# Seven-product matrix multiplies in a fused attention and FFN block: one operand of the second weight made later, and partial sums of the first product kept in PSUM

## The chip, the cores and the metric

The kernel runs on 1 core of one Trainium2 chip. The metric is the device time in microseconds (us) of one launch; it includes everything from the first load to the last store. A time is given as the median of several runs.

## What is computed

The reference is a block on a sequence of 2048 tokens of width 576, all in float32. Its inputs are normalized per token; one branch is linear attention with 32 heads of width 18, the other an FFN with a hidden width of 4608, and the branches are multiplied:

```python
xn = _layernorm(x)
q, k, v = split(xn @ wqkv)                  # 32 heads of width 18
phi = lambda t: where(t > 0, t + 1, exp(t)) + 1e-6
kv = einsum("bhsd,bhse->bhde", phi(k), v);  z = phi(k).sum over tokens
s = ((phi(q) @ kv) / (phi(q) . z + 1e-6)) @ wo
h = gelu(xn @ w1 + b1)                      # 576 -> 4608
g = silu(h @ w2 + b2)                       # 4608 -> 576
out = x + s * g
```

Most of the work, and the whole change, lies in the two FFN products `xn @ w1` and `h @ w2`.

## The kernel before, in words

**Float32 from pairs.** A matrix operand `t` is kept as a high part `hi`, a rounded copy of `t` in TensorE's fast float32 format, and a low part `lo = t - hi`. A product takes three matmuls: hi·hi, hi·lo, lo·hi. The high part is made by ScalarE (`set_hi`, L812, a cast; in the first stage `w2_hi`, L413), the low part by VectorE (`set_lo`, L815; for the first weight L874; in the first stage `w2_lo`, L418). Below, such a step is called a *cast* or *split*.

**Seven products in place of eight.** Both FFN products are cut into blocks of two by two and multiplied by a scheme of Strassen's kind: seven products M1 to M7 of sums of blocks, and additions on the results. Operands that are sums (of the inputs, the weights or the hidden values) are made by POOL, in place.

**Stages.** In the first stage (to about 150 us) the keys and values are projected, one tile of 128 tokens after the other (loop over `t`, 16 tiles), and in the gaps some operands of the weights are made and stored to DRAM: `w2_load`, `w2_sum`, `w2_hi`, `w2_lo`, `w2_store` (L392 to L423) make operands 5 and 6 of the second weight (`T_OPS`) for all 9 chunks. POOL makes the sum (L405), ScalarE the high part (L413), VectorE the low part (L418), and SP's queue stores both (L423). The second stage (to 283 us) does the queries and the attention output.

**The FFN stage** has 18 steps of the loop at L1511, called chunks here: 9 chunks of 512 hidden columns for the first half of the tokens, and the same 9 for the second half. In the first half the weights' operands are made and stored to DRAM; in the second they are loaded. A chunk has two *pairs* (class `Up`, L1129, each for 256 hidden columns and 1024 tokens) and then the down products (`product`, L1273). The very last chunk ends with plain products instead (`down_plain`, L1386).

**A pair** calls `step(i)` for the products in the order `UP` (L1453): 1, 6, 7, 5, 2, 3, 4. Each product is 7 matmuls of 512 columns (`mm`, L1140). Its results go through PSUM:

- `bank1` tiles (pool `psum1`, two buffers of one bank): `a` and `e`. `bank2` tiles (pool `psum`, three buffers of two banks): `b` and `zy`; only one bank of `b` is used.
- M1 goes to `a`; ScalarE copies it to SBUF (`m1_sb`, L1164). Later M2 adds onto it in `a`.
- VectorE makes `u1 = M6 + M1` (L1167) and `u2 = M7 + u1` (L1170) in SBUF, then M5 + u2 (L1173), M3 + M5 + u1 (L1180; M3 adds onto M5 in `e`) and M4 + u2 (L1184) in PSUM.
- Four GELUs by ScalarE (`gelu`, L1155) read the four sums and write the hidden blocks to SBUF. The block of the last GELU (`gelu(0, 1, ...)`) is needed for sums 7 and 5 of the second product's operands.

**The down products** run in the order 1, 2, 7, 4, 5, 3, 6 (`ORDER`), each as two *groups* of 12 matmuls of 288 columns on a `bank2` tile. M2 adds onto M1's tile, M4 onto M7's and M3 onto M5's, and VectorE adds each tile to the accumulator `macc` (L1292). So a chunk takes 4 + 8 = 12 `bank2` tiles from the three buffers, always in the same places: `b` and `zy` of the first pair take buffers 0 and 1, those of the second 2 and 0, the two groups of the first down product take 1 and 2, the next 0.

**Order of the work.** `in_order` (L59, entered at L1509) fixes VectorE, ScalarE, POOL and TensorE to the order in which the program issues instructions; SP's queue of DMAs is not named there. After each step of a pair and each group `at_step` (L1495) issues what the tables have planned for that step. A chunk has 28 steps (`NS`): 0 to 6 the first pair, 7 to 13 the second, 14 to 27 the groups. In the first half, `P1` and `P0` plan the first weight's operands; `PW2` (L1475) plans the high parts of the second weight's operands (2 at step 0, 1 at 1, 7 at 3, 4 at 5, 3 at 8), with the low part and the store to DRAM (`keep_op`, L806) one step later, and POOL's `sum7` (L1199) at step 0 and two `sum4` (L1202) at step 2. Operands 5 and 6 are loaded at steps 23 and 27 of the chunk before. `PH` (L1479) plans sums (POOL), high and low parts of the second product's left operands, made from the GELUs' blocks; the first of them are planned from step 7 on, beside the second pair. POOL's sums, the casts and the splits of one chunk thus share queues with the additions and the GELUs of its pairs. At the change from the first half to the second, three SiLU activations of accumulators (L1362) are planned for the first two steps.

Of the kernel before, what the change touches and what calls it, by code (L numbers as in the profile page):

```python
# [8 lines left out]
F32 = mybir.dt.float32  # L9
F32R = mybir.dt.float32r  # L10
# [5 lines left out]
P = 128  # L16
S = 2048
D = 576
HD = 288
# [25 lines left out]
def linear_attention_gated_ffn(ctx, tc, x, xT, wqkv, wo, w1, w1e, b1, w2, b2, out):  # L45
    nc = tc.nc
    SUB, MUL, ADD = ALU.subtract, ALU.mult, ALU.add
# [34 lines left out]
    def bank2(name):  # L82
        return psum.tile([P, 2, 512], F32, tag="pp", name=name)

    def bank1(name):
        return psum1.tile([P, 512], F32, tag="p1", name=name)
# [36 lines left out]
    w1_dram, w2_dram = {}, {}  # L123
# [262 lines left out]

    T_OPS = (5, 6)
    w2raw, w2op = {}, {}  # L390

    def w2_load(c):  # L392
        t = w2p.tile([P, 3, 2, HD], F32, tag="w2r", name=f"w2r{c}")
        nc.sync.dma_start(t.rearrange("p b a d -> p (b a d)"), w2[c][:, D:])
        w2raw[c] = t

    def w2_block(c, i):

        B11, B00, B01 = (w2raw[c][:, k] for k in range(3))
        return {5: (B00, B01, B00), 6: (B11, B11, B00)}[i]  # L400

    def w2_sum(j):
        c, i = j // 2, T_OPS[j % 2]
        dst, a, b = w2_block(c, i)
        nc.gpsimd.tensor_tensor(dst, a, b, op=SUB)  # L405

    def w2_hi(j):
        shape = [P, 2, 2, HD]
        if j % 4 < 2:
            w2op[j] = stw.tile(shape, F32R, tag="stw", name=f"w2o{j}")  # L410
        else:
            w2op[j] = w2p.tile(shape, F32R, tag="w2o", name=f"w2o{j}")
        nc.scalar.copy(w2op[j][:, 0], w2_block(j // 2, T_OPS[j % 2])[0])  # L413

    def w2_lo(j):
        c, i = j // 2, T_OPS[j % 2]
        t = w2op[j]
        nc.vector.tensor_tensor(t[:, 1], w2_block(c, i)[0], t[:, 0].bitcast(F32), op=SUB)  # L418

    def w2_store(j):  # L420
        c, i = j // 2, T_OPS[j % 2]
        w2_dram[c, i] = d = dram.tile([P, 2, 2, HD], F32, name=f"op_{c}_{i}")
        nc.sync.dma_start(d, w2op.pop(j).bitcast(F32))  # L423

# [32 lines left out]
    WE_SUMS = {2 * q + 1: q for q in range(WG)}  # L457
    W2_AT = (2, 4, 6, 8, 10, 11, 12, 13, 14)
    W2_LOADS = {0: 0, 1: 1, 3: 2, 5: 3, 7: 4, 9: 5, 11: 6, 12: 7, 13: 8}
    W2_SUMS = {t: (2 * c, 2 * c + 1) for c, t in enumerate(W2_AT)}  # L460

    class XSums:

# [18 lines left out]
        def tt(self, out, a, b, op):  # L482
            nc.vector.tensor_tensor(out, a.bitcast(F32), b.bitcast(F32), op=op)
# [24 lines left out]
        def sum4(self, k):  # L508
            self.tt(self.t, (self.h0, self.l0)[k][:, self.B], self.t, (SUB, ADD)[k])
# [615 lines left out]

    mid = md.tile([P, 5, 512], F32, name="mid")
    m1_sb, u1_sb, u2_sb = (mid[:, i] for i in range(3))

    class Up:  # L1129


        def __init__(self, n, w, xs):
            self.p, self.w = n % NP, w
            self.xb = xs

            self.a, self.b = bank1(f"a{n}"), bank2(f"b{n}")
            self.zy, self.e = bank2(f"zy{n}"), bank1(f"e{n}")
            self.g = {}

        def mm(self, ps, i, first=True):  # L1140
# [15 lines left out]
            self.g[n, b] = g  # L1156

        def step(self, i):
            A, B, E = self.a, self.b[:, 0, :], self.e
            Z, Y = self.zy[:, 0, :], self.zy[:, 1, :]  # L1160
            tt = nc.vector.tensor_tensor
            if i == 1:
                self.mm(A, 1)
                nc.scalar.copy(m1_sb, A)  # L1164
            elif i == 6:
                self.mm(B, 6)
                tt(u1_sb, B, m1_sb, op=ADD)  # L1167
            elif i == 7:
                self.mm(Z, 7)
                tt(u2_sb, Z, u1_sb, op=ADD)  # L1170
            elif i == 5:
                self.mm(E, 5)
                tt(B, E, u2_sb, op=ADD)  # L1173
                self.gelu(1, 1, B)
            elif i == 2:
                self.mm(A, 2, first=False)
                self.gelu(0, 0, A)
            elif i == 3:
                self.mm(E, 3, first=False)
                tt(E, E, u1_sb, op=ADD)  # L1180
                self.gelu(1, 0, E)
            else:
                self.mm(Y, 4)
                tt(Y, Y, u2_sb, op=ADD)  # L1184
                self.gelu(0, 1, Y)


    class W2:
# [10 lines left out]
        def sum7(self):  # L1199
            nc.gpsimd.tensor_tensor(self.src[7], self.src[3], self.src[7], op=SUB)  # L1200

        def sum4(self, k):  # L1202

            self.src[4] = t = self.src[2]
            nc.gpsimd.tensor_tensor(t, t, self.src[(7, 1)[k]], op=SUB)

        def plain(self, f):
            k = 2 - 2 * (f % 2)
# [16 lines left out]
    class HOps:  # L1225
# [224 lines left out]
        if i:  # L1450
            load_rest(0, REST_AT[i], 1, x_new[k][:, 4])

    UP = (1, 6, 7, 5, 2, 3, 4)  # L1453
    NS = 28


# [15 lines left out]
    )  # L1472


    PW2 = {2: 0, 1: 1, 7: 3, 4: 5, 3: 8}  # L1475
    W2_SUMS_NEXT = {5: 23, 6: 27}
    W2_SUMS_FIRST = {5: 6, 6: 10}
    W2_NEXT = {1: 15, 2: 17, 7: 19, 4: 21, 5: 23, 3: 25, 6: 27}
    PH = dict(  # L1479
        S={(7, 0): 7, (5, 0): 8, (6, 0): 11, (3, 0): 11, (7, 1): 13, (5, 1): 14, (6, 1): 15, (3, 1): 15},  # L1480
# [30 lines left out]
    for step in range(n_chunks):  # L1511
# [4 lines left out]
        if half == 0:  # L1516
            plan_w1(add, w1t[2 * step + 1], base, **P1)
            add(base, w2t[step].sum7)
            for k in range(2):
                add(base + 2, w2t[step].sum4, k)  # L1520
            for i, at in PW2.items():
                add(base + at, w2t[step].hi, i)
                add(base + at + 1, w2t[step].lo, i)
            if step == 0:
                for i, at in W2_SUMS_FIRST.items():
                    add(at, w2t[0].load, i)
        change = step == NC - 1
        if not plain:
            add(base + (11 if change else 7), load_we, 2 * step + 2)
# [1 line left out]
        if half == 0 and c < NC - 1:  # L1531
            add(base + 0, make, W1, w1t, 2 * step + 2)
            add(base + 4, make, W1, w1t, 2 * step + 3)
            add(base + 1, lambda n=2 * step + 2, base=base: plan_w1(add, w1t[n], base, **P0))
            make(W2, w2t, step + 1)
            add(base + 22, w2t[step + 1].load_raw)
            for i, at in W2_SUMS_NEXT.items():
                add(base + at, lambda i=i, n=step + 1: w2t[n].load(i))
        elif not plain:
            add(base + (11 if change else 7), make, W1Loaded, w1t, 2 * step + 2)  # L1540
            add(base + (11 if change else 14), load_six, 2 * step + 2)
            add(base + (16 if change else 14), make, W1Loaded, w1t, 2 * step + 3)
# [115 lines left out]
```

## Time and profile before

| | |
|---|---|
| Runs | 1098.13, 1102.75 and 1105.87 us; median 1102.75 us |
| Span of the profiled execution, first to last instruction | 1096.2 us |
| Time around that span, against the runs' median | 6.55 us |
| TensorE clock granted, mean over the span | 0.999 |
| First and second stage | 0 to 283 us |
| Chunks, first half of the tokens | 9, from 283.0 us |
| Chunks, second half of the tokens | 9, from 685.5 us; the last one ends in plain products |
| HBM read and written | 164.24 MB and 95.17 MB |
| DMA packets | 262.54 MB, mean 239 GB/s |

How to read the profile: PE is TensorE's matmuls, PEld its weight loads (they overlap), DVE is VectorE, ACT is ScalarE, POOL is GpSimd, SP is the engine that issues DMAs. `L1164` is line 1164 of the kernel before. A row of groups gives line, engine, operation, output `<-` inputs, shapes and the number of instructions, then busy us and mean ns of one, then the idle time of the engine before them and who ended it. A row of the timeline gives start in us, duration in us, engine, line, operation and tiles, and in brackets the engine's idle time before it. Matmuls are pipelined, so durations of single matmuls overlap; the time of a product is read from the length of a stretch.

### The profile page before, as it was taken

The page shows a single profiled execution, that of the slowest core. Times are in us where ns is not written, and L with a number is a line of the kernel's source. Part 1 is how long each engine was busy: PE and PEld are TensorE (multiplying, and loading weights), DVE is VectorE, ACT ScalarE, POOL GpSimd, SP SyncE. Part 2 cuts the span into 40 slices and gives each one's busy share as a digit, 9 for nine tenths or more (in the row PEclk, how much of TensorE's full clock was granted, in tenths as well). Part 3 has the DMA queues.
Part 4 walks back from the last instruction along what each step waited for, and adds up shares of the span by engine and source line. Part 5 has one row for each costly group of instructions (what it writes and reads, how often), then busy time and mean ns, then how long its engine had stood idle before and what let it go on. Part 6 is the DMA issues. An engine that isn't in the chain of part 4 may idle for free.

```text
span 1096.2 us, 18083 instructions
## 1 busy us (share of the span) xinstructions
PE 1088.2 (99%) x6702; PEld 1008.8 (92%) x6702; DVE 829.5 (76%) x1132; ACT 491.3 (45%) x844; POOL 471.5 (43%) x403
## 2 busy tenths in 40 slices
PE   9999999999999999999999999999999999999998
PEld 8999989999898998989989989899898998989987
DVE  7787748888798888888888888667475584764856
ACT  6555555555545455454453544524234243242442
POOL 3676434323546446464554553424234143242340
PEclk9999999999999999999999999999999999999999
DMA  7898834675959558486585769978676676767452
GB/s 248 264 274 274 309 137 149 206 248 186 333 221 350 182 220 322 160 320 224 189 332 175 284 237 400 391 248 289 215 241 219 210 231 212 238 219 224 126 184 87
DMA packets 88400, 262.54 MB, mean 239 GB/s; under 512 B 11894, under 2 KB 24182, under 8 KB 85624
## 3 DMA queue, kind: packets, MB, share of 16 engines
q1 hardware_dynamic: 88312, 261.38, 69.3%
q8 instruction: 53, 0.87, 0.3%
q14 instruction: 35, 0.29, 0.1%
HBM read 164.24 MB, written 95.17 MB: 237 GB/s over the span
## 4 chain that ended last, share of the span: by engine, by line
PE 99%; DVE 1%; ACT 0%; issue 0%; POOL 0%; DVEq 0%; POOLq 0%
PE pm L1286 35%; PE a L1147 10%; PE e L1147 10%; PE zy L1147 10%; PE pk L321 6%; PE pq L321 5%; PE ps_s L788 5%; PE b L1147 5%; PE pv L321 4%; PE pd L1402 2%; PE ps_kva L382 1%; PE ptp L770 1%; PE ps_kw L707 1%; PE warm L369 0%; DVE wkv_l L364 0%; PE ps_kvb L382 0%
## 5 line engine op out<-in xcount | busy, mean ns | idle before, releaser
L1292 DVE TENSOR_TENSOR macc<-pm,macc 128x576 f32<-128x576 f32 x218 | 163.9, 752 | 49.9 <-PE pm L1286 48.4
L812 ACT CAST h_h<-g 128x512 fp32r<-128x512 f32 x204 | 121.9, 621 | 132.7 <-PE pm L1286 131.5
L815 DVE TENSOR_TENSOR h_l<-g,h_h 128x512 fp32r<-128x512 f32 x204 | 161.8, 800 | 0.0
L1252 POOL TENSOR_TENSOR mid<-g 128x512 f32<-128x512 f32 x34 | 43.9, 1292 | 108.1 <-ACT g L1155 108.1
L1246 POOL TENSOR_TENSOR g<-g 128x512 f32<-128x512 f32 x34 | 54.9, 1616 | 49.5 <-DVE h_l L815 28.4
L1155 ACT ACTIVATE g<-b,b1c 128x512 f32<-128x512 f32 x36 | 24.8, 690 | 102.5 <-DVE b L1173 102.5
L1164 ACT COPY mid<-a 128x512 f32<-128x512 f32 x36 | 21.1, 585 | 95.3 <-PE a L1147 95.3
L858 POOL TENSOR_TENSOR w1raw<-w1raw 128x256 f32<-128x256 f32 x18 | 13.3, 737 | 116.8 <-ACT h_h L812 68.2
L1167 DVE TENSOR_TENSOR mid<-b,mid 128x512 f32<-128x512 f32 x36 | 24.8, 690 | 45.0 <-PE b L1147 41.8
L1374 POOL TENSOR_TENSOR fin1l<-fin1h,fin1l 128x288 f32<-128x288 f32 x8 | 6.5, 811 | 118.4 <-DMA fin1l<-s_dram 69.6
L1249 POOL TENSOR_TENSOR g<-g 128x512 f32<-128x512 f32 x34 | 55.2, 1623 | 2.7
L1147 PE MATMUL a<-h0r,wa 128*128 128x512 f32 x144 | 50.4, 390 | 0.0
L1147 PE MATMUL a<-xh,wa 128*128 128x512 f32 x144 | 50.4, 390 | 0.0
L815 DVE TENSOR_TENSOR h_l<-mid,h_h 128x512 fp32r<-128x512 f32 x34 | 48.8, 1436 | 1.2
L1155 ACT ACTIVATE g<-e,b1c 128x512 f32<-128x512 f32 x36 | 24.8, 690 | 51.9 <-DVE e L1180 51.9
L753 POOL TENSOR_TENSOR pbuf<-phiq,den 128x576 f32<-128x576 f32 x16 | 19.4, 1213 | 63.6 <-DVE den L752 63.6
L1243 POOL TENSOR_TENSOR g<-g 128x512 f32<-128x512 f32 x34 | 44.1, 1296 | 2.7
L1180 DVE TENSOR_TENSOR e<-e,mid 128x512 f32<-128x512 f32 x36 | 24.8, 690 | 22.3 <-PE e L1147 22.3
L1170 DVE TENSOR_TENSOR mid<-zy,mid 128x512 f32<-128x512 f32 x36 | 24.9, 691 | 19.8 <-PE zy L1147 19.8
L1173 DVE TENSOR_TENSOR b<-e,mid 128x512 f32<-128x512 f32 x36 | 25.2, 700 | 18.5 <-PE e L1147 17.4
L321 PE MATMUL pk<-wkv_h,xh 128*128 128x288 f32 (+1 forms) x160 | 38.2, 321 | 0.4 <-ACT xh L248 0.4
L321 PE MATMUL pk<-wkv_l,xh 128*128 128x288 f32 (+1 forms) x160 | 38.4, 321 | 0.0
(857 smaller groups left out, 3646.5 us busy)
## 6 DMA issues: line engine op xcount, KB each, us to landing
we<-we_dram SPq DMA_DIRECT2D x36, 448.0 KB
w2raw<-w SPq DMA_DIRECT2D x10, 1152.0 KB
op<-w2o SPq DMA_DIRECT2D x18, 576.0 KB
w1raw<-w SPq DMA_DIRECT2D x18, 512.0 KB
op_a<-wa SPq DMA_DIRECT2D x18, 512.0 KB
op_c<-wc SPq DMA_DIRECT2D x18, 512.0 KB
op_d<-wd SPq DMA_DIRECT2D x18, 512.0 KB
wc<-op_c SPq DMA_DIRECT2D x18, 512.0 KB
```

Source lines behind the costliest of these rows:

```text
L321: nc.tensor.matmul(ps[:, h, : ws.stop - ws.start], st, w[:, k, ws], start=(begin and i == 0), stop=(end and i == len(seq) - 1), skip_group ...
L788: nc.tensor.matmul(ps[:, h, :HD], st[:, k, :], w[:, k, h * HD : (h + 1) * HD], start=(i == 0), stop=(i == len(seq) - 1),)
L812: nc.scalar.copy(pair[0], src)
L815: eng.tensor_tensor(pair[1], src, pair[0].bitcast(F32), op=SUB)
L1147: nc.tensor.matmul(ps, st, mv, start=first and n == 0, stop=n == len(seq) - 1, skip_group_check=True,)
L1155: nc.scalar.activation(g, ps, AF.Gelu_apprx_tanh, bias=b1c[:, f : f + 1])
L1243: tt(src[5, pr], A(1, 0), A(1, 1), op=ADD)
L1246: tt(src[6, pr], src[5, pr], A(0, 0), op=SUB)
L1249: tt(src[3, pr], A(0, 1), src[6, pr], op=SUB)
L1252: tt(src[7, pr], A(0, 0), A(1, 0), op=SUB)
L1286: nc.tensor.matmul(ps[:, q, :HD], hs[p][st][:, cs], m[:, p, :], start=(n == 0 and i not in CHAIN), stop=(n == 5), skip_group_check=True,)
L1292: nc.vector.tensor_tensor(dst, src, dst, op=ADD)
```

## The change

Two things change. First, operand 6 of the second weight is not made in the first stage any more: the load there takes two blocks instead of three, only operand 5 is made, and one tile tag holds it. Operand 6 is made in the chunks of the first half: POOL makes it as `sum6` from operand 7, in place of a block, operand 4 then takes one subtraction (of operand 6) instead of two, and `PW2` casts 4 at step 6, 6 at step 7 and 3 at step 9. It is stored to DRAM there, and loaded from there in the second half as before.

Second, a pair's products come in the order 1, 2, 6, 5, 7, 3, 4. M6 and M7 add onto M1 in the bank `a`; ScalarE copies the bank after M1, after M6 (`u1`) and after M7 (`u2`), and copies M5 from `e`, into the place of M1's copy. VectorE's additions are four: M2 + m1, (M1+M6+M7) + m5, M3 + M5 + u1, M4 + u2. The `bank2` tiles are `bc` (bank B for M2, bank C for M4) and `z` (written by VectorE alone), in the places of `b` and `zy`.

```diff
     def w2_load(c):
-        t = w2p.tile([P, 3, 2, HD], F32, tag="w2r", name=f"w2r{c}")
-        nc.sync.dma_start(t.rearrange("p b a d -> p (b a d)"), w2[c][:, D:])
+        t = w2p.tile([P, 2, 2, HD], F32, tag="w2r", name=f"w2r{c}")
+        nc.sync.dma_start(t.rearrange("p b a d -> p (b a d)"), w2[c][:, 2 * D :])
...
+    def w2_sum(c):
+        B00, B01 = (w2raw[c][:, k] for k in range(2))
+        nc.gpsimd.tensor_tensor(B00, B01, B00, op=SUB)
...
-    W2_SUMS = {t: (2 * c, 2 * c + 1) for c, t in enumerate(W2_AT)}
+    W2_SUMS = {t: (c,) for c, t in enumerate(W2_AT)}
...
     m1_sb, u1_sb, u2_sb = (mid[:, i] for i in range(3))
+    m5_sb = m1_sb
...
-            self.a, self.b = bank1(f"a{n}"), bank2(f"b{n}")
-            self.zy, self.e = bank2(f"zy{n}"), bank1(f"e{n}")
+            self.a, self.e = bank1(f"a{n}"), bank1(f"e{n}")
+            self.bc, self.z = bank2(f"bc{n}"), bank2(f"z{n}")
...
             if i == 1:
                 self.mm(A, 1)
                 nc.scalar.copy(m1_sb, A)
+            elif i == 2:
+                self.mm(B, 2)
+                tt(B, B, m1_sb, op=ADD)
             elif i == 6:
-                self.mm(B, 6)
-                tt(u1_sb, B, m1_sb, op=ADD)
-            elif i == 7:
-                self.mm(Z, 7)
-                tt(u2_sb, Z, u1_sb, op=ADD)
+                self.mm(A, 6, first=False)
+                nc.scalar.copy(u1_sb, A)
+                self.gelu(0, 0, B)
             elif i == 5:
                 self.mm(E, 5)
-                tt(B, E, u2_sb, op=ADD)
-                self.gelu(1, 1, B)
-            elif i == 2:
-                self.mm(A, 2, first=False)
-                self.gelu(0, 0, A)
-            elif i == 3:
+                nc.scalar.copy(m5_sb, E)
+            elif i == 7:
+                self.mm(A, 7, first=False)
+                tt(Z, A, m5_sb, op=ADD)
+                nc.scalar.copy(u2_sb, A)
+                self.gelu(1, 1, Z)
+            elif i == 4:
+                self.mm(C, 4)
+                tt(C, C, u2_sb, op=ADD)
+                self.gelu(0, 1, C)
+            else:
                 self.mm(E, 3, first=False)
                 tt(E, E, u1_sb, op=ADD)
                 self.gelu(1, 0, E)
-            else:
-                self.mm(Y, 4)
-                tt(Y, Y, u2_sb, op=ADD)
-                self.gelu(0, 1, Y)
...
-        def sum4(self, k):
-
+        def sum6(self):
+            self.src[6] = t = self.src[1]
+            nc.gpsimd.tensor_tensor(t, self.src[7], t, op=ADD)
+
+        def sum4(self):
             self.src[4] = t = self.src[2]
-            nc.gpsimd.tensor_tensor(t, t, self.src[(7, 1)[k]], op=SUB)
+            nc.gpsimd.tensor_tensor(t, t, self.src[6], op=SUB)
...
-    UP = (1, 6, 7, 5, 2, 3, 4)
+    UP = (1, 2, 6, 5, 7, 3, 4)
...
-    PW2 = {2: 0, 1: 1, 7: 3, 4: 5, 3: 8}
-    W2_SUMS_NEXT = {5: 23, 6: 27}
-    W2_SUMS_FIRST = {5: 6, 6: 10}
+    PW2 = {2: 0, 1: 1, 7: 3, 4: 6, 6: 7, 3: 9}
...
-            for k in range(2):
-                add(base + 2, w2t[step].sum4, k)
+            add(base + 3, w2t[step].sum6)
+            add(base + 3, w2t[step].sum4)
...
-            for i, at in W2_SUMS_NEXT.items():
-                add(base + at, lambda i=i, n=step + 1: w2t[n].load(i))
+            add(base + 23, w2t[step + 1].load, 5)
```

More of the change, by code (lines that the diff above doesn't have):

```diff
@@ L385, in state, with w2_hi, w2_lo, w2_store @@
             )
-    T_OPS = (5, 6)
     w2raw, w2op = {}, {}
     def w2_load(c):
-        t = w2p.tile([P, 3, 2, HD], F32, tag="w2r", name=f"w2r{c}")
-        nc.sync.dma_start(t.rearrange("p b a d -> p (b a d)"), w2[c][:, D:])
+        t = w2p.tile([P, 2, 2, HD], F32, tag="w2r", name=f"w2r{c}")
+        nc.sync.dma_start(t.rearrange("p b a d -> p (b a d)"), w2[c][:, 2 * D :])
         w2raw[c] = t
[L397 to L410, printed above, removed]
-        else:
[L412 to L423, printed above, removed]
+    def w2_sum(c):
+        B00, B01 = (w2raw[c][:, k] for k in range(2))
+        nc.gpsimd.tensor_tensor(B00, B01, B00, op=SUB)
+    def w2_hi(c):
+        w2op[c] = w2p.tile([P, 2, 2, HD], F32R, tag="w2o", name=f"w2o{c}")
+        nc.scalar.copy(w2op[c][:, 0], w2raw[c][:, 0])
+    def w2_lo(c):
+        t = w2op[c]
+        nc.vector.tensor_tensor(t[:, 1], w2raw[c][:, 0], t[:, 0].bitcast(F32), op=SUB)
+    def w2_store(c):
+        w2_dram[c, 5] = d = dram.tile([P, 2, 2, HD], F32, name=f"op_{c}_5")
+        nc.sync.dma_start(d, w2op.pop(c).bitcast(F32))
     we = {}
@@ L1158, in step @@
         def step(self, i):
-            A, B, E = self.a, self.b[:, 0, :], self.e
-            Z, Y = self.zy[:, 0, :], self.zy[:, 1, :]
+            A, E, Z = self.a, self.e, self.z[:, 0, :]
+            B, C = self.bc[:, 0, :], self.bc[:, 1, :]
             tt = nc.vector.tensor_tensor
@@ L1181, in step @@
                 self.gelu(1, 0, E)
-            else:
-                self.mm(Y, 4)
-                tt(Y, Y, u2_sb, op=ADD)
-                self.gelu(0, 1, Y)
     class W2:
@@ L1524, in linear_attention_gated_ffn @@
             if step == 0:
-                for i, at in W2_SUMS_FIRST.items():
-                    add(at, w2t[0].load, i)
+                add(6, w2t[0].load, 5)
         change = step == NC - 1
```

## The prediction

> **What bounds the kernel now.** I read the page first: the busy table, then the chain that ended last.
>
> ```profile
> span 1096.2 us, 18083 instructions
> PE 1088.2 (99%) x6702; PEld 1008.8 (92%) x6702; DVE 829.5 (76%) x1132; ACT 491.3 (45%) x844; POOL 471.5 (43%) x403
> PE 99%; DVE 1%; ACT 0%; issue 0%; POOL 0%; DVEq 0%; POOLq 0%
> ```
>
> TensorE is the bound, and the chain is TensorE nearly throughout. A busy PE could still be a stretched one, so I read who PE waited for, and then a steady chunk by its stages: first pair, second pair and down products in the first half, the two pairs in the second. The last two rows are the first stage, and a short stretch that a rival needs.
>
> ```profile
> PE warm L369 <- POOL ident masks.py:199: 2.0, 1, 2.0
> PE pk L321 <- ACT xh L248: 0.4, 1, 0.4
> PE pv L321 <- DVE wkv_l L364: 0.2, 1, 0.2
> ```
>
> ```profile
> core 0: us, PE busy (x) PEld busy (x) DVE busy (x) ACT busy (x) POOL busy (x), PEclk, DMA share, GB/s
> 461.88:473.01 11.13, 11.13 (x51) 9.20 (x50) 9.10 (x12) 5.53 (x10) 7.17 (x6) 1.00 0.95 350
> 473.01:484.14 11.13, 11.13 (x51) 9.20 (x49) 9.75 (x14) 6.71 (x12) 5.62 (x4) 1.00 1.01 377
> 484.14:506.59 22.45, 22.45 (x169) 22.40 (x168) 20.28 (x28) 9.05 (x16) 10.63 (x10) 1.00 0.37 129
> 774.80:785.93 11.13, 11.13 (x51) 9.20 (x50) 3.54 (x5) 2.58 (x4) 2.48 (x4) 1.00 0.55 177
> 785.93:797.07 11.14, 11.14 (x51) 9.20 (x50) 6.58 (x9) 5.11 (x10) 5.65 (x4) 1.00 0.73 241
> 0.00:150.00 150.00, 147.38 (x915) 142.56 (x915) 111.31 (x167) 83.08 (x158) 85.20 (x92) 1.00 0.86 271
> 155.00:162.00 7.00, 6.94 (x25) 3.05 (x23) 3.60 (x7) 4.58 (x10) 1.41 (x1) 1.00 0.13 43
> ```
>
> PE waits for 2.6 us in the whole span, all at its start. In the chunks it never waits, at a clock of 1.00, and a pair takes 11.13 us whether VectorE is busy for 9.10 (first half) or 3.54 us (second half). So one product takes 11.13 / 7 = 1.59 us, and a down group of 12 matmuls 22.4 / 14 = 1.60 us. The change takes no matmul away. It can gain almost nothing; the question is whether its shorter waits reach PE.
>
> **What is taken away or moved.** Operand 6 leaves the first stage:
>
> ```profile
> L405 POOL TENSOR_TENSOR w2r<-w2r 128x576 f32<-128x576 f32 x18 | 28.8, 1598 | 15.6 <-DVE phik L340 8.5 <-DMA w2r<-w 6.4
> L418 DVE TENSOR_TENSOR w2o<-w2r,w2o 128x576 fp32r<-128x576 f32 x18 | 19.1, 1098 | 0.2
> L413 ACT CAST w2o<-w2r 128x576 fp32r<-128x576 f32 x18 | 11.5, 672 | 2.5 <-POOL w2r L405 2.5
> ```
>
> Half of each goes: 9 x 1.6 = 14.4 us of POOL, 9 x 1.1 of VectorE, 9 x 0.67 of ScalarE, nine stores and a third of nine loads. All of it lies beside PE's 147.38 busy us of 150, and no wait of PE names a weight-two tile or a DMA there: I take 0, bounds 0 and -2.6 us (all of PE's waits). ScalarE's and VectorE's halves come back in the nine first-half chunks, with a store in eight; the POOL sums there stay two. SP drops nine loads that stood behind the last down product; the new store waits for the low part of operand 6, and what queues behind it on SP is for the next chunk, over 20 us away. I take 0 for both; were the operand's cast and split on PE's path, they would cost 9 x (0.67 + 1.1) = 16 us, but they are walked through with their queues below. The missing VectorE addition (0.69 us a pair) is worth nothing by itself, by the two halves' equal 11.13 us.
>
> **What is added on PE's path.** M1, M6 and M7 now add up in one bank, so M6 must wait for the copy of M1, M7 for the copy of M1+M6, and M3 (same bank as M5) for the copy of M5. Each has one product, 1.59 us, of cover.
>
> ```profile
> L1164 ACT COPY mid<-a 128x512 f32<-128x512 f32 x36 | 21.1, 585 | 95.3 <-PE a L1147 95.3
> ```
>
> A copy starts at most 0.28 us after its product (787.80 below, in a pair from 785.93 whose M1 takes 1.59) and takes 0.585: 0.9 of 1.59 us, so covered wherever ScalarE is free. It is not free at the start of the second pair of a first-half chunk. ScalarE's and VectorE's order there, before:
>
> ```profile
> 474.79 0.66 ACT L812 CAST w__5376<-w2raw 128x576 fp32r<-128x576 f32 x1
> 475.40 0.69 ACT L1155 ACTIVATE g<-zy,b1c 128x512 f32<-128x512 f32 x1
> 475.98 0.58 ACT L1164 COPY mid<-a 128x512 f32<-128x512 f32 x1
> ```
>
> ```profile
> 471.58 1.98 DVE L815 TENSOR_TENSOR w__5342<-w2raw,w__5342 128x576 fp32r<-128x576 f32 x1
> 473.48 0.69 DVE L1180 TENSOR_TENSOR e<-e,mid 128x512 f32<-128x512 f32 x1
> 474.68 0.69 DVE L1184 TENSOR_TENSOR zy<-zy,mid 128x512 f32<-128x512 f32 x1
> 481.54 1.63 DVE L815 TENSOR_TENSOR h_l<-mid,h_h 128x512 fp32r<-128x512 f32 x1
> 483.70 1.18 DVE L815 TENSOR_TENSOR h_l<-g,h_h 128x512 fp32r<-128x512 f32 x1
> 484.80 0.68 DVE L1184 TENSOR_TENSOR zy<-zy,mid 128x512 f32<-128x512 f32 x1
> ```
>
> ```profile
> 469.49 3.45 POOL L1205 TENSOR_TENSOR w2raw<-w2raw 128x576 f32<-128x576 f32 x2
> 481.04 1.59 POOL L1246 TENSOR_TENSOR g<-g 128x512 f32<-128x512 f32 x1 [2.20 <-ACT g L1155]
> 485.52 0.69 ACT L1155 ACTIVATE g<-zy,b1c 128x512 f32<-128x512 f32 x1 [0.36 <-DVE zy L1184]
> ```
>
> A VectorE split that meets a POOL sum ends about 0.6 us after the sum: 473.56 after POOL's 472.94, 483.17 after 482.63. That holds the last addition of the first pair to 474.68, and its GELU to 475.40. The change keeps these POOL sums and this split where they are. Then it puts the high part of operand 4 (0.66 us, before this ahead of the GELU) between that GELU and the copy of M1.
>
> *First stall.* Steps on ScalarE are 0.58 apart: operand 4 at 475.98, the copy at 476.56, done at 477.15. M6 is due third, at 473.01 + 2 x 1.59 = 476.19. With 0.06 for the release it starts at 477.2: **1.0 us** of stall. Bounds: 0.4 if operand 4 cost nothing (the copy ends at 476.56 even now), 1.3 if it costs its full length and the handover more.
>
> *Second stall.* As I read the pool, a new tile of two banks takes a buffer when the last use of the old tile is over. Before, the second down group of a chunk took the buffer of B, free early; now it takes the one of B and C, and C's GELU is the last thing of the pair. The trace cannot show this wait, as nothing reached it. The group is due 1.60 us after M4's end. In the second half, undisturbed:
>
> ```profile
> 786.16 0.70 DVE L1184 TENSOR_TENSOR zy<-zy,mid 128x512 f32<-128x512 f32 x1 [0.89 <-PE zy L1147]
> 786.95 0.69 ACT L1155 ACTIVATE g<-zy,b1c 128x512 f32<-128x512 f32 x1 [0.96 <-DVE zy L1184]
> 787.80 0.59 ACT L1164 COPY mid<-a 128x512 f32<-128x512 f32 x1 [0.16 <-PE a L1147]
> ```
>
> the GELU ends at 787.64, 1.71 us after M4 (785.93). In the second pairs of before it ends at 486.21, 2.07 after 484.14, behind a split of 1.18. So a second-half chunk stalls 0.17 us (1.71 + 0.06 - 1.60); bounds 0 and 0.53. I take the low value, since there the earlier GELUs let the splits go before.
>
> In a first-half chunk I walk the queues on. PE: M6 ends at 478.79, then M5 480.38, M7 481.97, M3 483.56, M4 485.15, first down group 486.75. ScalarE: operand 6 to 477.7, a cast to 478.3, copy of M1+M6 479.02 to 479.61 (M7 due 480.38), GELU to 480.2, operand 3 to 480.8, a cast to 481.3, copy of M5 to 481.8 (M3 due 481.97). VectorE, through with operands 4 and 6 by 479.9: low part of operand 3 480.8 to 481.55, two splits to 482.76, the addition after M7 to 483.37, a split that POOL holds to 484.48, the addition after M3 to 485.09, a split that POOL holds to 486.2, the addition after M4 to 486.81; its GELU ends at 487.54. The group can start at 487.6: **0.85 us**. Bounds 0.17 and, if one more POOL sum gets ahead, 1.2.
>
> The copy of M1+M6+M7 shares its bank with an addition. Two engines reading one bank are put in a row, as here:
>
> ```profile
> L648 ACT COPY sums_k<-ps_kva x1: 572/572/572, 150.8 to 150.8; 31x504 f32<-31x504 f32 x1
>   DVE kvz L645: 3.7, 1
> ```
>
> so it ends near 484.0, before M4's addition at 486.1 needs it: 0.
>
> *Two single places.* At the half change three SiLUs and a table load stand on ScalarE at the pair's start, and in the first chunk a table load:
>
> ```profile
> 690.74 1.17 ACT L1362 ACTIVATE macc<-macc 128x1152 f32<-128x1152 f32 x1 [0.72 <-DVE macc L1302]
> 691.93 1.28 ACT L1155 ACT_TABLE_LOAD   x1
> 289.17 1.28 ACT L1155 ACT_TABLE_LOAD   x1
> ```
>
> Half change (pair from 685.4, five chunks of 44.71 after 461.88): the copy of M1+M6 waits for the SiLU and ends at 692.4, M7 was due at 691.8: 0.6; then load, GELU and copy of M5 end at 694.9, M3 due at 694.0: 0.9. First chunk (from 283.0): the copy of M1+M6 to 288.6, load, GELU, cast and copy of M5 to 291.4, M3 due at 291.0: 0.5. Together 2.0, bounds 0 and 3.5.
>
> **The sum.** 9 x (1.0 + 0.85) = 16.7; 8 x 0.17 = 1.4; 2.0; the last chunk, whose down products have 24 matmuls before the buffer in question, 0. In all 20.1 us on the span of 1096.2, so 1116.3. The span lies 6.55 under the runs' median of 1102.75; with the same 6.55 around it, **1123 us**, 1.8% slower. Ends: 9 x (0.4 + 0.17) - 2.6 = +2.5 and 9 x 2.5 + 8 x 0.53 + 3.5 = +30, so 1105 to 1133.
>
> **The rivals.** (A) *Not slower:* VectorE's split of operand 7 gets the port before POOL's two sums, as ScalarE reaches that operand 0.8 us sooner (an earlier GELU went from in front of it). Then additions follow their products as at 786.16, the copy of M1 ends near 475.8, ahead of 476.19, and the second stall falls to some 0.3: 9 x 0.3 + 1.4 + 2.0 = 6, 1109 us, no change that can be told. It decides from the point where the copy is 1.0 us sooner than I have it. Against it: the addition after M7 now stands ahead of both splits, and POOL's sums start at 469.49, before that addition is due. Chance 0.15. (B) *Banks are handed on one by one:* the group's first five matmuls go into B's bank, which buys 0.67 us; 9 x (1.0 + 0.18) + 2.0 = 12.6, 1115 us. Chance 0.10. (C) *The copy of M5 is late too:* its margin before M3 is 0.17 us in a first-half chunk; half a us over it in nine chunks adds 4.5, and the second-half bound of 0.53 another 2.9: 1130 us. Chance 0.08. (D) *The clock falls.* Rows: the first transposes, straight after idle time, took 421 ns against 272 later.
>
> ```profile
> L238 PE MATMUL pt0a<-ident,xn x4: 421/421/421, 6.3 to 7.0; 128*128 128x128 f32 x4
> L238 PE MATMUL pt1a<-ident,xn x4: 272/273/274, 15.9 to 16.2; 128*128 128x128 f32 x4
> ```
>
> If the array ran at half speed from the first stall to the second (9.5 us), nine chunks would lose 86 us: 1209. Against it: at 155 to 162 us, where weights load for only 3.05 of 7.00 us, the clock is 1.00. Chance 0.03. This is a rule of the Trainium skill (TensorE: Matmul & The Clock Gate, "A second HAM failure mode: psum-queue depth-cycling"): small idle times between groups of matmuls, made by cycling through banks, let the clock swing between half and full. By that page's window of about 3.4 us, 18 stalls would cost an estimated 31 us, 1154. (E) *Faster*, by something that I do not see: the waits of PE hold 2.6 us, 0.2%. Chance 0.02.
>
> **Chances.** The forecast itself has 0.62. About 1% is what a measurement of this kernel can tell from no change. Slower by more: the forecast, B, C and D, 0.83. Within 1%: A, 0.15. Faster: E, 0.02. The range from 1109 to 1132 takes in A's price, B and most of C.
>
> **What would show it.** PE waits on ScalarE's copy of M1 in nine chunks, about 1.0 us each, and on a GELU before the second down group in seventeen, 0.85 and 0.17; a first-half chunk of 46.6 us against 44.71, a second-half one of 44.8; copies of M1 that end near 15.3 us into a chunk instead of 14.7. Wrong would be chunks of 44.7 us in the first half, or a wait on any DMA.

## The result, and the profile after

The changed kernel takes **1110.41 us** (median of 4 runs, 1110.18 to 1110.62). The kernel before, run beside it, has a median of 1100.82 us (4 runs, 1098.13 to 1105.87). The ratio is **1.0078** [1.0048, 1.0107]: slower, by less than half of the 1.8% that was forecast. (The four runs of before scatter over 7.7 us; against its later medians, below, the change costs 1.1%.) The profiled execution took 1110.38 us; its span is 12.5 us longer than that of before.

The head of the page after, and the whole list of what TensorE waited for (total us, times, longest):

```profile
span 1108.7 us, 18087 instructions
PE 1092.9 (99%) x6702; PEld 1007.6 (91%) x6702; DVE 788.5 (71%) x1096; ACT 545.5 (49%) x952; POOL 453.1 (41%) x394
```

```profile
PE a L1135 <- ACT mid L1152: 6.4, 9, 0.8
PE warm L369 <- POOL ident masks.py:199: 2.0, 1, 2.0
PE e L1135 <- ACT mid L1162: 0.9, 2, 0.6
PE pk L321 <- DVE xh L251: 0.5, 1, 0.5
PE a L1135 <- ACT mid L1158: 0.4, 1, 0.4
```

L1152 is ScalarE's copy of M1, L1158 that of M1+M6, L1162 that of M5. So the first stall is there, nine times, and so are the two single places. No `pm` tile (the PSUM tile of a down group) stands in the list: the second stall isn't there.

Where the 12.5 us lie shows in the table by stretches: the first two stages together, the nine first-half chunks, and the chunk after the half change, first of the kernel before:

```profile
0.00:283.04 283.04, 280.37 (x1891) 271.09 (x1892) 216.48 (x321) 156.19 (x283) 132.93 (x135) 1.00 0.72 231
283.04:685.47 402.43, 402.43 (x2396) 367.23 (x2395) 349.17 (x456) 193.75 (x333) 206.80 (x167) 1.00 0.71 263
685.47:730.14 44.67, 44.67 (x269) 40.80 (x267) 31.95 (x42) 19.05 (x28) 15.02 (x10) 1.00 0.94 352
```

and of the kernel after:

```profile
0.00:282.48 282.48, 279.87 (x1890) 271.00 (x1891) 199.40 (x312) 151.23 (x274) 117.07 (x126) 1.00 0.68 203
282.48:696.94 414.46, 407.14 (x2396) 366.42 (x2395) 347.76 (x447) 226.41 (x396) 209.09 (x167) 1.00 0.71 256
696.94:743.18 46.24, 45.24 (x268) 40.63 (x267) 29.36 (x40) 22.00 (x34) 14.36 (x10) 1.00 0.90 328
```

The first half takes 12.0 us more, the half change 1.6 more, the first two stages 0.6 less, and what is left of the span 0.5 less. A steady first-half chunk of after, stage by stage, and the two pairs of a second-half chunk:

```profile
466.73:477.86 11.13, 11.13 (x51) 9.20 (x50) 8.68 (x11) 7.08 (x13) 7.12 (x6) 1.00 0.92 345
477.86:490.09 12.23, 11.47 (x51) 9.12 (x50) 9.80 (x14) 8.57 (x16) 5.76 (x4) 1.00 0.96 346
490.09:512.78 22.69, 22.62 (x170) 22.41 (x168) 20.53 (x28) 9.26 (x16) 10.86 (x10) 1.00 0.39 128
787.83:798.96 11.13, 11.13 (x51) 9.20 (x50) 2.86 (x4) 4.15 (x7) 2.79 (x4) 1.00 0.62 195
798.96:810.10 11.14, 11.14 (x51) 9.20 (x50) 5.40 (x8) 6.77 (x13) 5.18 (x4) 1.00 0.69 228
```

Against 11.13, 11.13 and 22.45 before: the second pair has lost **1.10 us**, the down products **0.24**, and the second half nothing. The clock is 1.00 everywhere.

The second pair's 1.10 us, in the timeline of after (start, duration):

```profile
474.47 1.42 POOL L1194 TENSOR_TENSOR w2raw<-w2raw 128x576 f32<-128x576 f32 x1
475.98 1.76 POOL L1198 TENSOR_TENSOR w2raw<-w2raw 128x576 f32<-128x576 f32 x1
...
476.37 1.98 DVE L802 TENSOR_TENSOR w__5314<-w2raw,w__5314 128x576 fp32r<-128x576 f32 x1
478.28 0.68 DVE L1174 TENSOR_TENSOR e<-e,mid 128x512 f32<-128x512 f32 x1
478.88 0.67 DVE L861 TENSOR_TENSOR wd<-w1raw,wd 128x512 fp32r<-128x512 f32 x1
479.48 0.68 DVE L1170 TENSOR_TENSOR bc<-bc,mid 128x512 f32<-128x512 f32 x1
...
480.20 0.69 ACT L1143 ACTIVATE g<-bc,b1c 128x512 f32<-128x512 f32 x1 [0.51 <-DVE bc L1170]
480.79 0.66 ACT L799 CAST w__5360<-w2raw 128x576 fp32r<-128x576 f32 x1
481.35 0.58 ACT L1152 COPY mid<-a 128x512 f32<-128x512 f32 x1
...
481.99 0.96 PE L1135 MATMUL a<-s,w 128*128 128x512 f32 x3 [0.76 <-ACT mid L1152]
```

Read it from the end. M6 starts at 481.99, behind the copy of M1 (to 481.93). The copy stands behind operand 4's cast, the cast behind the GELU of C, that behind its addition (L1170). On VectorE this addition stands behind a split of the first weight (`wd`) and the addition after M3 (L1174), and both behind the split of operand 7 (`w__5314`), which took 1.98 us; POOL's sum, beside it, ran until 477.74. M6 was due two products after the start of the pair, at 477.86 + 3.18 = 481.04, so it is 0.95 us late; the other 0.15 of the 1.10 are lost behind the restart.

### The profile page after: what moved, and what is told of

Its sections match the earlier page's. It is cut to its first block, busy times and chain, and to the rows that moved or that the text cites. A ratio compares the mean times of both kernels' runs of the same rounds, so it can differ in the third digit from the quotient of the medians.

```text
span 1108.7 us, 18087 instructions
## 1 busy us (share of the span) xinstructions
PE 1092.9 (99%) x6702; PEld 1007.6 (91%) x6702; DVE 788.5 (71%) x1096; ACT 545.5 (49%) x952; POOL 453.1 (41%) x394
## 4 chain that ended last, share of the span: by engine, by line
PE 91%; DVE 3%; ACT 2%; issue 2%; DMA 2%; POOL 0%; SPq 0%; DVEq 0%; ACTq 0%; POOLq 0%
PE pm L1279 35%; PE a L1135 13%; PE e L1135 8%; PE bc L1135 8%; PE pk L321 6%; PE pq L321 5%; PE ps_s L775 5%; PE pv L321 4%; PE pd L1395 2%; DMA op<-w 2%; PE ps_kva L382 1%; PE ptp L757 1%; PE ps_kw L694 1%; DVE e L1174 1%; DVE bc L1170 1%
## 5 line engine op out<-in xcount | busy, mean ns | idle before, releaser
L1285 DVE TENSOR_TENSOR macc<-pm,macc 128x576 f32<-128x576 f32 x218 | 164.2, 753 | 53.5 <-PE pm L1279 52.4
L802 DVE TENSOR_TENSOR h_l<-g,h_h 128x512 fp32r<-128x512 f32 x204 | 157.8, 777 | 15.7 <-ACT h_h L799 15.3
L1152 ACT COPY mid<-a 128x512 f32<-128x512 f32 x36 | 21.1, 587 | 95.2 <-PE a L1135 93.9
L1165 DVE TENSOR_TENSOR z<-a,mid 128x512 f32<-128x512 f32 x36 | 25.1, 698 | 51.8 <-PE a L1135 47.7
L1143 ACT ACTIVATE g<-bc,b1c 128x512 f32<-128x512 f32 x72 | 49.8, 691 | 18.1 <-DVE bc L1170 18.0
L1155 DVE TENSOR_TENSOR bc<-bc,mid 128x512 f32<-128x512 f32 x36 | 25.0, 694 | 41.6 <-PE bc L1135 40.2
L1158 ACT COPY mid<-a 128x512 f32<-128x512 f32 x36 | 21.1, 585 | 54.7 <-PE a L1135 54.7
L1166 ACT COPY mid<-a 128x512 f32<-128x512 f32 x36 | 21.1, 587 | 41.0 <-DVE z L1165 41.0
L775 PE MATMUL ps_s<-kw_h,th 128*128 128x288 f32 x160 | 35.5, 303 | 0.0
L802 DVE TENSOR_TENSOR h_l<-mid,h_h 128x512 fp32r<-128x512 f32 x34 | 34.1, 1004 | 1.9 <-ACT h_h L799 1.9
L1135 PE MATMUL a<-s,w 128*128 128x512 f32 x108 | 28.6, 400 | 6.4 <-ACT mid L1152 6.4
L321 PE MATMUL pq<-wq_h,xh 128*128 128x288 f32 x160 | 34.8, 299 | 0.0
```

The costliest lines, as they stand in the source:

```text
L321: nc.tensor.matmul(ps[:, h, : ws.stop - ws.start], st, w[:, k, ws], start=(begin and i == 0), stop=(end and i == len(seq) - 1), skip_group ...
L775: nc.tensor.matmul(ps[:, h, :HD], st[:, k, :], w[:, k, h * HD : (h + 1) * HD], start=(i == 0), stop=(i == len(seq) - 1),)
L802: eng.tensor_tensor(pair[1], src, pair[0].bitcast(F32), op=SUB)
L1135: nc.tensor.matmul(ps, st, mv, start=first and n == 0, stop=n == len(seq) - 1, skip_group_check=True,)
L1143: nc.scalar.activation(g, ps, AF.Gelu_apprx_tanh, bias=b1c[:, f : f + 1])
L1285: nc.vector.tensor_tensor(dst, src, dst, op=ADD)
```

## The experiments

All were timed against the kernel before, in three series whose medians of it are 1098.13 (the first four kernels), 1098.23 (the next four) and 1098.05 us (the last two). "Chunk" is a steady first-half chunk: 44.71 us before, 46.04 after.

| kernel | span | median | ratio to before, 95% interval | chunk |
|---|---|---|---|---|
| second part alone (e1) | 1110.5 | 1112.25 | 1.0122 [1.0097, 1.0147] | 46.38 |
| first part alone (e2) | 1101.3 | 1103.00 | 1.0036 [1.0021, 1.0050] | 45.17 |
| operand 7's low part late (e3) | 1099.7 | 1101.54 | 1.0025 [1.0012, 1.0038] | 44.98 |
| operand 4's parts late (e4) | 1103.9 | 1105.57 | 1.0063 [1.0042, 1.0083] | 45.50 |
| e3, Z's buffer released last (e5) | 1105.8 | 1107.87 | 1.0075 [1.0057, 1.0093] | 45.53 |
| e1, two POOL sums late (e6) | 1105.4 | 1106.97 | 1.0065 [1.0044, 1.0086] | 45.82 |
| e3, operand 3 early (e7) | 1097.0 | 1098.50 | 0.9996 [0.9985, 1.0006] | 44.65 |
| e7, single places mended (e8) | 1094.3 | 1096.24 | 0.9972 [0.9962, 0.9981] | 44.65 |
| first part alone, mended (e9) | 1094.7 | 1097.42 | 0.9992 [0.9975, 1.0008] | 44.65 |
| second part alone, mended (e10) | 1095.3 | 1097.00 | 0.9987 [0.9978, 0.9997] | 44.71 |

### Each part by itself

The second part alone leaves `Up` and its order as in the kernel before; the first part alone leaves the second weight's operands as there:

```
 e1:  UP = (1, 6, 7, 5, 2, 3, 4)      PW2 = {2: 0, 1: 1, 7: 3, 4: 6, 6: 7, 3: 9}
 e2:  UP = (1, 2, 6, 5, 7, 3, 4)      PW2 = {2: 0, 1: 1, 7: 3, 4: 5, 3: 8}
```

> The changed kernel without its first part: operand 6 of the second weight is made in the chunks, the first product is summed as before. My theory (TensorE loses its time because M6 must wait for ScalarE's late copy of M1): no wait on a copy, chunks of 44.7 us, at most the 0.23 us before the fourth down product that the changed kernel has; the chunks start 0.55 us sooner, so a span of 1095.6 to 1098. Rival 1 (the extra sum, cast, split and store of operand 6 in the first-half chunks are what costs): chunks of 46.0 us here as well, span about 1108. Rival 2 (both parts cost, about half each): 1102.

> The changed kernel without its second part: M1, M6 and M7 are summed in one bank with ScalarE's copies, operands 5 and 6 of the second weight are made in stage 1 as before, so that operand 4's cast stands ahead of the GELU and not behind it. My theory: the second pair's copy of M1 ends at 14.7 us into a first-half chunk, as it did before; M6 is due at 14.3, so 0.4 us are lost in each of nine chunks, with the first chunk's 0.55 and the half change's 1.54 and no shorter first stage: span 1101 to 1104. Rival 1 (operand 6's making is what costs): 1096 to 1098. A rival 3 (a sum in one bank costs TensorE a fixed time in any chunk, wherever the copy comes): 1.0 us per chunk again, span 1108.

The first part alone came out as my theory has it, at 1101.3. The second pair and the down products of a chunk (from the table by stretches):

```profile
474.81:486.40 11.59, 11.38 (x50) 9.06 (x49) 10.48 (x13) 7.91 (x14) 5.17 (x4) 1.00 0.95 376
486.40:508.87 22.47, 22.47 (x170) 22.43 (x169) 20.09 (x29) 9.27 (x16) 10.47 (x9) 1.00 0.37 126
```

0.46 us in the pair, none of the 0.24 in the down products: those 0.24 come with the second part.

The second part alone was missed, and badly: it is the slowest kernel of all, slower than both parts together. TensorE's waits there are others:

```profile
PE pm L1276 <- DVE h_l L802: 4.2, 9, 0.5
PE pm L1276 <- DVE macc L1282: 2.2, 8, 0.3
...
PE e L1134 <- DVE b L1160: 1.8, 9, 0.2
```

```profile
489.13 1.58 POOL L1236 TENSOR_TENSOR g<-g 128x512 f32<-128x512 f32 x1 [3.45 <-DVE h_l L802]
...
489.48 1.78 DVE L802 TENSOR_TENSOR h_l<-mid,h_h 128x512 fp32r<-128x512 f32 x1
```

None is a copy; all three are VectorE, late in the second pair, with a split among its work that takes 1.78 us beside a POOL sum. So rival 1 is half right: making operand 6 in the chunk costs, but what it costs hangs on the other part. I read it so, and no run isolates it: with the first product summed as before, VectorE has the additions after M6, M7 and M5 to do in a chain; the change's first part takes one away and gives ScalarE the copies. With that part the same operand 6 costs 0.87 us a chunk (46.04 against 45.17: the later cast and the 0.24) instead of 1.67.

### The copy of M1

```
 e3:                 add(base + at, w2t[step].hi, i)
-                    add(base + at + 1, w2t[step].lo, i)
+                    add(base + (6 if i == 7 else at + 1), w2t[step].lo, i)
 e4:
-    PW2 = {2: 0, 1: 1, 7: 3, 4: 6, 6: 7, 3: 9}
+    PW2 = {2: 0, 1: 1, 7: 3, 6: 7, 4: 8, 3: 9}
```

> The changed kernel with one VectorE instruction moved: the low part of the second weight's operand 7, which meets POOL's sums, goes behind the first pair's last addition. My theory: the last addition, its GELU and the copy of M1 come some 1.5 us sooner, the copy ends near 13.6 us into a first-half chunk as in the second half, M6 waits for nothing: 8 x 1.03 + 0.6 = 8.8 us less, span 1100, chunks of 44.7 to 45.0 us. Rival 3: unchanged, 1108.7. Rival 4 (only the cast of operand 4 ahead of the copy matters): unchanged, since it stays where it is.

> The changed kernel with the high and low part of the second weight's operand 4 made two steps later, behind the copy of M1. My theory: the copy starts with the end of the GELU at 14.05 us into the chunk, not at 14.62, and the stall falls from 1.03 to 0.45 us in nine chunks, 5.1 us less: span 1103.6. Rival 4 (the cast alone makes the stall): the stall is gone, 1100. Rival 3: unchanged, 1108.7.

Both fell where my theory put them (1099.7 for 1100, 1103.9 for 1103.6), and rivals 3 and 4 are out: the sum in one bank has no fixed price, and the cast accounts for about half. In the first of the two:

```profile
474.54 0.69 DVE L1170 TENSOR_TENSOR bc<-bc,mid 128x512 f32<-128x512 f32 x1
475.14 0.74 DVE L802 TENSOR_TENSOR w__5314<-w2raw,w__5314 128x576 fp32r<-128x576 f32 x1
...
476.41 0.59 ACT L1152 COPY mid<-a 128x512 f32<-128x512 f32 x1
```

```profile
474.17:485.34 11.17, 11.17 (x51) 9.23 (x50) 9.24 (x13) 8.00 (x16) 5.79 (x4) 1.00 0.98 349
485.34:508.02 22.68, 22.57 (x170) 22.37 (x169) 20.52 (x28) 9.26 (x16) 10.84 (x10) 1.00 0.42 143
```

The same split takes 0.74 us instead of 1.98, behind the addition instead of ahead of it; the copy ends at 477.0, 0.35 us before M6 is due (474.17 + 3.18), and the pair is back at 11.17. The Trainium skill (SBUF — State Buffer, "SBUF: two separate sides") calls VectorE's and GpSimd's common port an exclusive lock: the operation that starts first holds it to its end and the other blocks. The 1.98 and the 0.74 us of one and the same split agree with that.

### The second stall, made on purpose

```
             self.p, self.w = n % NP, w
+            self.last = n % 2 == 1
...
-                self.gelu(1, 1, Z)
+                if not self.last:
+                    self.gelu(1, 1, Z)
...
                 self.gelu(0, 1, C)
+                if self.last:
+                    self.gelu(1, 1, Z)
```

> The kernel with the low part of operand 7 late, and in the second pair of each chunk the GELU of Z moved behind the GELU of C, so that Z's buffer is the last to be released and not B and C's. It asks where my second stall went. Theory: a new tile takes the buffer whose last use stands first in the program, so here the second group of the first down product must wait for the GELU of C: due 1.6 us after M4, that GELU ends 2.3 us after it, 0.7 to 0.85 us in each first-half chunk and 0.1 to 0.15 in a second-half one, span 1106 to 1108. Rival A (banks are handed on singly): the group's first five matmuls go into B's bank and cover 0.67 us, span 1100 to 1101. Rival B (buffers are taken in turn, whatever was released): the same buffer as without the change, span 1099.7.

The span, 1105.8, is 0.2 us under the theory's range and far from both rivals'. The wait is where the theory puts it:

```profile
PE pm L1283 <- ACT g L1144: 5.3, 9, 0.6
```

```profile
464.97:510.49 45.52, 44.92 (x269) 40.80 (x268) 37.37 (x51) 24.81 (x44) 23.75 (x19) 1.00 0.68 242
828.68:873.51 44.83, 44.83 (x268) 40.81 (x267) 25.24 (x36) 17.63 (x30) 14.29 (x13) 1.00 0.71 220
```

A first-half chunk takes 0.54 us more than without the GELU's move (45.52 for 44.98), a second-half one 0.18 (44.83 for 44.65). In the first half the new wait takes in the one before the fourth down product, 0.3 us, which is gone: some 0.85 us by itself. The second down group of the first of these two chunks shows the wait:

```profile
488.87 0.69 ACT L1144 ACTIVATE g<-bc,b1c 128x512 f32<-128x512 f32 x1 [0.36 <-DVE bc L1172]
...
489.61 0.54 PE L1283 MATMUL pm<-w__5281,h_h 128*128 128x288 f32 x2 [0.60 <-ACT g L1144]
```

The group starts at 489.61, right behind C's GELU (to 489.56). These two sizes are close to the 0.85 and 0.17 us of the prediction: the stall was priced rightly and put on the wrong buffer.

### What is left, mended

```
 e6:      S={(7, 0): 7, (5, 0): 8, (6, 0): 13, (3, 0): 14, ...        # in place of 11 and 11
 e7:      PW2 = {2: 0, 1: 1, 7: 3, 4: 6, 6: 7, 3: 8}                  # operand 3: 8 in place of 9
 e8:      self.copy = nc.vector.tensor_copy if n == 2 * NC else nc.scalar.copy
          ...
              add(1, lambda: nc.scalar.activation(early, b1c[:, 0:1], AF.Gelu_apprx_tanh))
```

> The kernel that makes operand 6 in the chunks but sums the first product as before, with two POOL sums (first down operands 6 and 3 of the first pair) put behind the second pair, so that VectorE's splits there no longer meet them. Theory (that kernel's 1.67 us per chunk is VectorE held up by POOL, not the making of the operand as such): the wait for a split before the first down product and the one before the fourth go, the one of M3 stays: chunks of 45.0 us, span 1097 to 1100. Rival (VectorE simply has too much to do in the second pair): chunks stay above 46 us, span 1108 or more.

> The kernel with the low part of operand 7 late, and the parts of operand 3 of the second weight made one step sooner, where ScalarE and VectorE stand idle. Theory (the 0.28 us before the fourth down product is VectorE's chain of splits and additions, shifted as a whole, behind a cast of operand 3 that ScalarE reaches late): it goes, 9 x 0.28 = 2.5 us less, chunks of 44.7 us, span 1097.2. Rival (that wait is set by the additions after M3 and M4, which wait for TensorE, or by POOL's sums): unchanged, 1099.7.

> The kernel with operand 7's low part late and operand 3 early, and both single places mended: a GELU of one column ahead of the first chunk's copies loads the table early, and at the half change the copies of M1+M6 and of M5 go to VectorE. Theory: 0.55 and 1.54 us less than without these two, span 1095.1, some 0.1% under the kernel before. If the copies' lateness were not due to the SiLUs and the table load, 1097.2.

The sums moved in e6 are POOL's for left operands 6 and 3 of the down products, those made from the first pair's blocks. It came out between its two expectations: chunks of 45.82, where 45.0 was expected. The wait of the first down product for a split and the one before the fourth nearly go; M3's stays (as expected: the second pair takes 11.59 us); 0.3 us appear before the second down product, for an eviction that stands behind the same splits. One POOL sum, that of operand 5, still meets a split there (the split of operand 7 takes 1.78 us again). So POOL is part of that kernel's cost, and not all of it.

The other two fell as my theory has them, 0.2 and 0.8 us below: operand 3's cast, ahead of the GELU of B instead of behind it, takes the wait off the fourth down product, and with the two single places mended TensorE waits for nothing in any chunk. The whole list of its waits, and a first-half chunk beside the one after the half change:

```profile
PE warm L369 <- POOL ident masks.py:199: 2.0, 1, 2.0
PE pk L321 <- DVE xh L251: 0.7, 1, 0.7
```

```profile
460.99:505.63 44.64, 44.64 (x268) 40.78 (x267) 38.05 (x51) 24.78 (x44) 23.43 (x19) 1.00 0.69 246
684.22:728.87 44.65, 44.65 (x269) 40.78 (x268) 30.65 (x42) 21.06 (x32) 14.35 (x10) 1.00 0.94 353
```

Its time is 0.9972 [0.9962, 0.9981] of the kernel before, **faster**, and it has the lowest median of all. The 0.28% has the upward scatter of before's runs in it; by the medians (1096.24 and 1098.23) it is 0.18%, by the spans 1.9 us or 0.17%. With every stall of the change mended, that is what the change is worth. Of the 1.9 us 0.8 lie in the chunks: 44.65 for 44.71 in the first half, 44.65 for 44.67 in the second. Before, the second matmul of the fourth down product starts 0.21 us after the first (at 493.93 in the chunk from 461.88) where 0.13 is usual; in e8 that gap is gone. The other 1.1 us lie in the first two stages and in the last chunk, and no run says what made them.

> The first half of the change alone (sums in one bank, ScalarE's copies, four additions), operand 6 made in stage 1 as before, with operand 7's low part late and both single places mended. Theory (the change takes nothing off TensorE's path, its stalls were all of its effect): chunks of 44.65 us, a first stage as before, span 1094.3 to 1095.0, time within 0.3% of the kernel with both halves. Rival (stage 1's lighter work is what puts that one 2 us under the kernel before): 1096 or more.

> The second half of the change alone (operand 6 made in the chunks, the first product summed as before), with operand 7's low part late and operands 4, 6 and 3 in steps 5, 6 and 8. Theory (its 1.67 us per chunk come from the places of the casts and splits in the queues): chunks of 44.7 us, span 1094.5 to 1096.5. Rival (without the addition that the first half saves, VectorE has too much to do there): chunks of 45.3 us or more, span above 1101.

A first-half chunk of the first part alone, and one of the second part alone:

```profile
461.10:505.74 44.64, 44.64 (x268) 40.78 (x267) 37.32 (x50) 24.37 (x43) 23.11 (x19) 1.00 0.67 246
461.46:506.18 44.72, 44.72 (x269) 40.81 (x268) 40.04 (x53) 21.94 (x38) 24.21 (x19) 1.00 0.69 246
```

Each part alone can be mended too, to spans of 1094.7 and 1095.3, within 1 us of both together. So the second part alone need not cost 1.67 us a chunk, and that rival falls. The lighter first stage shows no gain of its own: e9, which has operand 6 in that stage, takes 0.3 us more than e8 in the span, and the end of the second stage lies between 282.3 and 283.0 us in all kernels, whichever way (282.55 in e9, 282.95 in e6). The medians of the three (1096.2 to 1097.4) are too close, with their intervals, to rank the parts.

## Why the prediction was wrong, step by step

**Right: the bound, and that nothing could be gained.** TensorE stays at 99%, it takes as many matmuls as before, and the removed stage-1 work shows in no time: the 0.6 us between the two profiles is no more than the scatter of the end of the second stage among all kernels, and e8 and e9, which differ in that work and in the operand's place, differ by 0.3 in the span.

**Right: the first stall.** 1.0 us a chunk by the queues of ScalarE; the pair lost 1.10. The mechanism is shown by e3, which frees the split, and by e4, which moves only operand 4's cast and split and leaves 0.46 us, near the lower bound of 0.4; the chain from POOL's sum to M6 is the one that was walked. That POOL's sums stay where they are is not quite so: the tables have them one step later, but they start 7.74 us into the chunk for 7.61, and the split meets them as before. The copy of M1+M6+M7 waits for the addition on the same bank in all 36 pairs, as expected, and holds nothing up. In a pair that is not held (second half) the copy is in time, as said.

**Right: the two single places.** 0.5 in the first chunk and 1.5 at the half change were forecast; e8 mended both, the first chunk fell by 0.7 us (45.28 in e7 to 44.60) and the half-change chunk by 46.24 - 44.65 = 1.6. Its span fell by 2.7 us where 2.1 were expected; the rest lies in the first two stages. A copy of M5 that is late in other chunks (rival C) does not occur.

**Wrong: the second stall, and this is the step that failed.** "As I read the pool, a new tile of two banks takes a buffer when the last use of the old tile is over", and then "now it takes the one of B and C". The first half of the sentence holds, the second does not follow from it. The trace after shows the group (due at 490.09 + 1.60) running through C's GELU:

```profile
491.68 0.42 PE L1279 MATMUL pm<-w__5281,h_h 128*128 128x288 f32 x2
491.94 0.29 PE L1279 MATMUL pm<-w__5281,h_l 128*128 128x288 f32 x1
492.07 0.69 PE L1279 MATMUL pm<-w__5281,h_h 128*128 128x288 f32 x4
...
491.69 0.69 ACT L1143 ACTIVATE g<-bc,b1c 128x512 f32<-128x512 f32 x1 [0.36 <-DVE bc L1170]
```

The GELU that reads `bc` ends at 492.38, the group's first matmul starts at 491.68. I had taken the buffers in turn, in the order in which they were asked for (`bc` before `z`). They come back in the order in which their last uses stand in the program, and there Z's GELU stands before C's. In the kernel before, both readings give the same buffer, so its trace could not tell them apart; e5, which on top of e3 swaps the two GELUs of the second pair and nothing else, does. It rules out rival B as well (banks handed on singly, 1115): with the buffer of B and C in play, B's bank alone let nothing start. The step put 9 x 0.85 + 8 x 0.17 = 9.0 of the 20.1 us into the sum; measured in the kernel after: 0.

**Missed: 0.24 us before the fourth down product.** The walk ended with the first down group. Behind it, VectorE's evictions are late as a whole:

```profile
499.01 0.74 DVE L1285 TENSOR_TENSOR macc<-pm,macc 128x576 f32<-128x576 f32 x1
...
499.54 0.29 PE L1279 MATMUL pm<-w__5314,h_l 128*128 128x288 f32 x1
499.90 0.50 PE L1279 MATMUL pm<-w__5360,h_h 128*128 128x288 f32 x2
```

The fourth product's first matmul, due 0.13 us after 499.54, starts at 499.90, after the eviction (the addition to `macc`, L1285) that ends at 499.75. Operand 3's cast, reached by ScalarE behind the GELU of B, is what shifts them: e7 moves it and the 0.3 us go.

**Wrong: what lies around the span.** I added the 6.55 us between the profiled span of before and the median of three runs. The later medians of before lie at 1098.05 to 1098.23, 1.9 us over that span, and after has 1110.38 - 1108.7 = 1.7 us around its own, as has every run with a span on record (1.7 to 1.8). The runs of before scatter upwards from 1097.1, and a profile that fell on a low one was added to a median of high ones: 6.55 - 1.7 = 4.9 us too much. With 20.1 - 9.0 + 9 x 0.24 - 1.1 (first two stages, and the rest of the span) = 12.2 and with 1.7 around it, the sum would have been 1110.1. So of the terms of 1123 the second stall is 9.0 us too much and what lies around the span 4.9; the rest is together some 1 us too little. Against the median of 1098.1 the change as made costs 1110.4 / 1098.1, **1.1%**; the ratio of 1.0078 has the first three runs of before in it.

**Rival A** (not slower) names 1109 us, close to what was measured, by a mechanism that was not at work: operand 7's split did not get ahead of POOL's sums, and the first stall is there in full. Only e3 made that so. The stated range reaches down to 1109 for that price alone, so that 1110.4 falls inside it is luck; and by its ratio, under 1%, the result lies where only rival A, with 0.15, had put it. **Rival D**, the clock: the granted clock is 1.00 in the second pair, where TensorE stands idle for about 1 us in the 46 of a chunk. No run shows the swing between half and full clock that the Trainium skill (TensorE: Matmul & The Clock Gate, "A second HAM failure mode: psum-queue depth-cycling") tells of; idle times of this length, this far apart, did not bring it here.

## What to carry to other kernels

When a sum moves from a vector engine into the accumulator, the engine that copies the running sum out becomes part of the matmul's path: list everything that stands ahead of that copy in its queue, back to what holds the first of them. Which buffer a new tile gets is a question of whose last use comes first in the program, and is worth settling before a wait is priced on it. Two edits to one queue do not add: here the parts alone cost 0.46 and 1.67 us a chunk and together 1.33, and moving a few casts and splits by one or two steps took all of it back.

## What the runs showed that I had not expected

- **The wait list understates a stall.** It gives 6.4 us for nine waits on the copy of M1, 0.71 each, while the pair is 1.10 longer. The modelled end of a matmul lies 0.39 us after its start where the next one follows 0.23 after, so the first part of a stall (0.16 us) counts as busy, and in the stall shown above the second matmul behind it starts 0.34 us after the first instead of 0.23. PE's busy time rose by 4.7 us with no matmul more. Stretches between the starts of the same products give the true loss.
- **The scatter of the runs went with operand 6's place.** In the three series 9 of 58 runs of before lie above 1101 us, up to 1106.3 (mean granted clock 0.996 to 0.998, the others 0.998 to 1.000), and so does one of 11 of e9, which makes operand 6 in the first stage as well. Each kernel that makes it in the chunks has its runs within 1.3 us of one another (61 runs in nine kernels). The first part alone, e2, has 7 runs within 1.1 us, so this isn't proof; which transfer or wait makes the long runs was not profiled and stays open.
